# Experts 0 to 3 of a mixture of experts on one core: down-projection between the halves of the next up-projection, and GELU's rounding by halves

## The chip, the core and the metric

The kernel runs on 1 core of one Trainium2 chip. The time is the device time of one execution in microseconds (us), the median of several runs. The engines are named as in the profile: PE (TensorE; PEld are its weight loads), DVE (VectorE), ACT (ScalarE), POOL (GpSimd) and SP (SyncE, which issues most DMAs).

## The reference, cut to what matters

The output is a gated sum of two branches over the same 2048 tokens of width 448: a Fourier mixing branch, and a mixture of 8 experts of which each token takes its best 2. The change touches the expert branch alone.

```python
h = _gelu(jnp.einsum("nd,edf->nef", xt, w1))      # up-projection, F = 1792
y = jnp.einsum("nef,efd->ned", h, w2)             # down-projection
out = jnp.einsum("ne,ned->nd", cw, y)             # cw: weights of the best 2, else 0
return g * a + (1 - g) * b
```

## The kernel before

**Capacities.** Only routed tokens are computed. The experts are sorted by load, and expert e of that order gets a fixed capacity, `CAPS` = 576, 544, 544, 544, 512, 512, 512, 496 tokens. Experts 0 to 3 have more than 512, so a row of them doesn't fit one PSUM bank. They are `NQ` = 4 in number.

**Jobs.** The hidden width is cut into 14 pieces of 128, so `jobs` lists 112 pairs (e, f), f = 0 to 13, numbered u = 14 e + f. `up(u)` computes the 128 hidden features of job u for all tokens of expert e: 11 matmuls into a PSUM tile `acc`, with 32-bit values split in a rounded part (`hi`, `XH`) and what rounding left (`lo`, `XL`): XH and XL by hi, then XH by lo. Experts 0 to 3 take this in two halves of 288 (expert 0; 256 and 320 for job 0) or 272 tokens, experts 4 to 7 in one go. ACT turns each half into `g` by GELU. Then the DVE writes `gh`, g rounded (L756, a CAST), and `gl`, what that left of it (L757, a subtraction), both over the first 512 tokens at once. Of the tokens beyond 512, expert 0 writes their remainder into gh (L764), and experts 1 to 3 copy g into `rest` (L762).

`down(u)` adds job u's part to the outputs of expert e: for every tile c of 128 tokens three matmuls of 448 columns into the PSUM tile `Y[c]` (gh by `up`, gh by `dn`, gl by `up`, where up and dn are the two parts of w2's rows). Tokens beyond 512 are a fifth tile: in expert 0 two matmuls, in experts 1 to 3 `few`, which collects 6 or 8 jobs and runs 8 narrow matmuls (L807). With the last job of an expert `combine` scales each tile of Y (DVE for even c, ACT for odd) and POOL adds it to the output by an indirect DMA.

**The order.** PE, DVE, ACT and SP run their instructions in the order in which the code gives them out. The loop (L1034 to L1053) has for each u: `turn_due` (gathered tokens of the next expert into XH and XL), `prep(u + 2)` (hi and up by ACT at L205, lo and dn by DVE at L210, then the fetch of job u + 5's weights by SP), routing work in the first steps (`advance`), `stage` (transposes of gathered tokens, L646, and new gathers on POOL), then `up(u + 1)`, `down(u)`, and `side_work` (checks of the DFT matrices on the DVE at L874, blends, sends). So the PE does all of up(u + 1) and then all of down(u); job u's gh and gl are needed one step after up(u). W (hi, lo) is used by up, V (up, dn) by down. `acc` has 3 buffers, g 2, gh and gl 3.

Of the kernel before, what the change touches and what calls it, by code (L numbers as in the profile page):

```python
# [10 lines left out]
F32R = mybir.dt.float32r  # L11
# [4 lines left out]
OP = mybir.AluOpType  # L16
AX = mybir.AxisListType

P = 128
# [3 lines left out]
DX = 512  # L23
# [5 lines left out]
CMAX = max(CAPS)  # L29
FULL = 4  # L30
RMAX = CMAX - FULL * P
# [9 lines left out]
NQ = P // Q  # L41
# [21 lines left out]
def r32(ap):  # L63
    return ap.bitcast(F32)


def tiles_of(cap):
    return [min(P, cap - c * P) for c in range((cap + P - 1) // P)]
# [3 lines left out]
def tile_kernel(ctx: ExitStack, tc: tile.TileContext, xt, xrows, xplain, wg, whid, cq, cw, cspec, edge, refs, wquad, whall, cgen, wcat, out):  # L72
    nc = tc.nc
    te, ve, se, gp, sp = nc.tensor, nc.vector, nc.scalar, nc.gpsimd, nc.sync
# [3 lines left out]
    stream = ctx.enter_context(tc.tile_pool(name="stream", bufs=3))  # L78
# [85 lines left out]
    def clear(i):  # L164
        if i == 0:
            rt["zero"] = mp.tile([P, D], F32, name="yt", bufs=1)
            ve.memset(rt["zero"], 0.0)
        if i < NT + NCT:
            sp.dma_start(out[i * P : (i + 1) * P, :], rt["zero"])
# [9 lines left out]
    jobs = [(e, f) for e in range(E) for f in range(NF)]  # L179
    RAW, W, V, owner = {}, {}, {}, {}  # L180
    rt = {}
# [16 lines left out]
    def apart(e):  # L198
        return CAPS[e] - FULL * P == Q
# [16 lines left out]
    def prep(k):  # L216
        if k < len(jobs):
            upper(k)
            lower(k)
# [237 lines left out]
    def advance(n=1):  # L457
        for _ in range(n):
            next(route, None)
# [225 lines left out]
    def turn_due(e, step, lag, pace):  # L685
        c = due(e, step - lag - 1, pace)
        if c is not None:
            turn(e, c)

    def stage(e, step, lag, pace):  # L690
        c = due(e, step - lag, pace)
        if c is not None:
            blocks(e, c)
        c = due(e, step, pace)
        if c is not None:
            gather(e, c)
# [30 lines left out]
    mp = late.enter_context(tc.tile_pool(name="mp", bufs=2, side="right"))  # L727
    UP, GH, Y, REST = 0, {}, {}, {}
    last = len(jobs) - 1

    def up(u):
        e, f = jobs[u]
        hi, lo = W[u]
        cap = CAPS[e]
        rem = max(0, cap - FULL * P)
        g = mp.tile([P, CMAX], F32, name="g")
        nh = 1 if cap <= 512 else 2
        cut = 2 * P if u == 0 else cap // nh
        for hf in range(nh):
            cs = slice(hf * cut, cap if hf == nh - 1 else cut)  # L740
            n = cs.stop - cs.start
            acc = ps.tile([P, 512], F32, name="acc")
            part = lambda w, x, c: (w[:, c * P : (c + 1) * P], x[e][:, c, cs])
            steps = [part(hi, XH, c) for c in range(NC - 1)] + [part(hi, XL, c) for c in range(NC - 1)]
            steps += [part(hi, XH, NC - 1)] + [part(lo, XH, c) for c in range(NC)]
            for s, (a, b) in enumerate(steps):
                te.matmul(acc[:, :n], a, b, start=s == 0, stop=s == len(steps) - 1)  # L747
            se.activation(g[:, cs], acc[:, :n], AF.Gelu_apprx_tanh)  # L748
        if u == last:
            gh, gl = (stream.tile([P, DX], F32R, name=n) for n in ("hi", "lo"))  # L750
        else:
            gh = mp.tile([P, CMAX + RMAX], F32R, name="gh", bufs=3)
            gl = mp.tile([P, FULL * P], F32R, name="gl", bufs=3)
        main = cap - rem
        top = main if apart(e) else cap
        ve.tensor_copy(gh[:, :top], g[:, :top])  # L756
        ve.tensor_tensor(gl[:, :main], g[:, :main], r32(gh[:, :main]), OP.subtract)  # L757
        if apart(e):
            if f in LOTS:
                rt["rest"] = mp.tile([P, NF - LOTS[1], Q], F32, name="rest", bufs=2)  # L760
            REST[u] = rt["rest"][:, f - max(b for b in LOTS if b <= f)]
            ve.tensor_copy(REST[u], g[:, main:cap])  # L762
        elif rem:
            ve.tensor_tensor(gh[:, cap : cap + rem], g[:, main:cap], r32(gh[:, main:cap]), OP.subtract)  # L764
        GH[u] = (gh, gl)

    def down(*us):
        e = jobs[us[0]][0]
        tl = tiles_of(CAPS[e])
        if jobs[us[0]][1] == 0:  # L770
            for c in range(len(tl)):
                Y[c] = psy.tile([P, 512], F32, name=f"y{BANKS[c]}")
        sent = []
        turns = [(c, u) for c in range(len(tl)) for u in us]
        if len(us) == 4:
            turns[3:5] = turns[4:2:-1]
        for c, u in turns:
            f, n = jobs[u][1], tl[c]
            if c == FULL and apart(e):
                few(e, u, sent)  # L780
                continue
            m = n if c < FULL else 2 * n
            cs = slice(c * P, c * P + m)
            wh, wl = (w[:, :D] for w in V[u])
            gh, gl = GH[u]
            steps = [(gh[:, cs], wh), (gh[:, cs], wl)]
            if c < FULL:
                steps.append((gl[:, cs], wh))
            for s, (a, b) in enumerate(steps):
                te.matmul(Y[c][:m, :D], a, b, start=f == 0 and s == 0, stop=f == NF - 1 and s == len(steps) - 1)  # L790
            if f == NF - 1:
                combine(e, c, n, sent)
        for u in us:
            del W[u], V[u], GH[u]

    def few(e, u, sent):
        f = jobs[u][1]
        if f + 1 not in LOTS:
            return
        lot = range(u - f + max(b for b in LOTS if b <= f), u + 1)  # L800
        for i in range(0, len(lot), NQ):
            group = lot[i : i + NQ]
            wide = NQ // len(group)
            for j in range(NQ):
                v = group[j // wide]
                cs = slice(j % wide * (D // wide), (j % wide + 1) * (D // wide))
                te.matmul(Y[FULL][j * Q : (j + 1) * Q, cs], REST[v], RAW[v][1][:, cs], start=f < LOTS[1] and i == 0, stop=f == NF - 1 and i + NQ >= len(lot), tile_position=(0, j * Q))  # L807
        for v in lot:
            del RAW[v], REST[v]
        if f == NF - 1:  # L810
            rt["rear"] = Y[FULL], sent
# [16 lines left out]
    def combine(e, c, n, sent):  # L828
        wt = rt["wgt"][:n, e, c : c + 1]
        ys = mp.tile([P, D], F32, name="ys", bufs=NCT)  # L830
        if c == FULL:
            yt = mp.tile([P, D], F32, name="yt", bufs=1)
            ve.tensor_copy(yt[:n], Y[c][n : 2 * n, :D])
            ve.tensor_tensor(yt[:n], Y[c][:n, :D], yt[:n], OP.add)
            ve.tensor_scalar(ys[:n], yt[:n], wt, None, op0=OP.mult)
        elif c % 2 == 0:
            ve.tensor_scalar(ys[:n], Y[c][:n, :D], wt, None, op0=OP.mult)
        else:
            se.activation(ys[:n], Y[c][:n, :D], AF.Copy, scale=wt)  # L839
        scatter(e, c, n, ys, sent)  # L840
# [190 lines left out]

    advance(2)
    up(UP)
    for u in range(UP, last):  # L1034
        e, f = jobs[u]
        plan = (e + 1, f - 1, 2, 2) if e else (1, f - 6, 2, 1)
        turn_due(*plan)
        prep(u + 2)
        if u < UP + SIDE:
            advance(2)  # L1040
            clear(2 * (u - UP))
            clear(2 * (u - UP) + 1)
        if u == last - NF - 1:
            tc.keep_in_program_order(gp.drain())
        if u == UP + SIDE:
            for _ in route:
                pass
            ck = late.enter_context(tc.tile_pool(name="ck", bufs=2, side="right"))
        stage(*plan)
        up(u + 1)  # L1050
        if u < last - 3:
            down(u)
        side_work(u - UP)  # L1053
    down(*range(last - 3, last + 1))
    order.close()
    late.close()
# [63 lines left out]
    with tc.For_i(0, n_a) as j:  # L1120
# [3 lines left out]
        for h in range(2):  # L1124
            hf = full.tile([P, 2 * D], F32, name="hf")
# [133 lines left out]
```

## Time and profile before

| | us |
|---|---|
| median of 3 runs (637.31 to 637.5) | 637.49 |
| the profiled execution | 637.86 |
| its span, first to last instruction | 635.9 |
| PE busy in it | 625.9 |
| DVE busy in it | 506.9 |
| ACT busy in it | 248.5 |

The profiled execution is one run; what lies around the span in it is 637.86 - 635.9 = 1.96 us. A busy time says how long an engine had something in hand, not that it was the limit; the chain of work that ended last tells which engine set the end.

### The profile page before, as it was taken

How to read it: one execution, taken by the hardware profiler on the slowest of the kernel's cores; microseconds unless marked ns; L12 is line 12 of the kernel's file. 1: busy time of each engine (PE TensorE's matmuls, PEld its weight loads, DVE VectorE, ACT ScalarE, POOL GpSimd, SP SyncE). 2: the span in 40 equal slices, each digit the busy share in tenths (PEclk: the TensorE clock that was granted, in tenths of full speed). 3: DMA queues.
4: the chain of work that ended last, by engine and by line, in shares of the span. 5: the costliest groups of instructions: out<-in, count | busy, mean ns of one | idle time of the engine just before them, and what ended most of it. 6: DMA issues, size and time to landing. Idle time of an engine off the chain costs nothing.

```text
span 635.9 us, 11090 instructions
## 1 busy us (share of the span) xinstructions
PE 625.9 (98%) x3721; PEld 563.8 (89%) x3721; DVE 506.9 (80%) x1258; ACT 248.5 (39%) x504; POOL 205.1 (32%) x194
## 2 busy tenths in 40 slices
PE   9999999999999999999999999999999999999994
PEld 5999999998998989989899788888888888888884
DVE  7889797689987899779898799988997788555560
ACT  2553233343344434353343534433343434534440
POOL 1210074554144141443340443432331442141123
PEclk9999999999999999999999999999999999999998
DMA  8546454795766865596566767779456737766755
GB/s 346 183 149 210 155 184 140 245 238 192 237 207 160 257 226 197 197 262 196 176 243 234 229 170 244 266 234 276 136 183 195 152 115 150 166 136 145 156 74 65
DMA packets 52319, 122.78 MB, mean 193 GB/s; under 512 B 7488, under 2 KB 32208, under 8 KB 50208
## 3 DMA queue, kind: packets, MB, share of 16 engines
q1 hardware_dynamic: 40944, 101.94, 47.2%
q0 software_dynamic: 11168, 20.00, 18.2%
q8 instruction: 31, 0.51, 0.3%
q14 instruction: 32, 0.26, 0.1%
q10 hardware_dynamic: 144, 0.07, 0.0%
HBM read 105.89 MB, written 16.08 MB: 192 GB/s over the span
## 4 chain that ended last, share of the span: by engine, by line
PE 94%; issue 3%; POOL 1%; DVE 1%; POOLq 0%; ACT 0%; DVEq 0%; ACTq 0%
PE acc L747 45%; PE y L790 42%; PE y L807 1%; PE acc L512 1%; PE y L555 1%; POOL out L843 1%; PE y L474 1%; PE y L116 1%; PE acc L453 0%; POOL out L995 0%; PE acc L404 0%; PE y L669 0%; PE acc L669 0%; POOLq L1028 0%; PE acc L373 0%
## 5 line engine op out<-in xcount | busy, mean ns | idle before, releaser
L748 ACT ACTIVATE g<-acc 128x272 f32<-128x272 f32 (+4 forms) x168 | 78.0, 467 | 318.2 <-issue 178.9
L637 POOL DMA_INDIRECT xg<-xrows,piece x115 | 120.5, 1048 | 226.2 <-DVE xq L646 154.3
L790 PE MATMUL y<-up,gh 128*128 128x448 f32 (+1 forms) x458 | 167.7, 366 | 0.1
L790 PE MATMUL y<-dn,gh 128*128 128x448 f32 (+1 forms) x458 | 167.6, 366 | 0.0
L747 PE MATMUL acc<-XH,hi 128*128 128x272 f32 (+4 forms) x672 | 163.8, 325 | 0.0
L790 PE MATMUL y<-up,gl 128*128 128x448 f32 (+1 forms) x444 | 162.7, 366 | 0.0
L747 PE MATMUL acc<-XH,lo 128*128 128x272 f32 (+4 forms) x672 | 134.9, 322 | 0.0
L747 PEld LDWEIGHTS acc<-XH,hi 128*128 128x128 f32 x672 | 115.2, 188 | 11.2 <-ACT hi L205 1.8
L747 PEld LDWEIGHTS acc<-XH,lo 128*128 128x128 f32 x672 | 105.9, 188 | 8.4
L756 DVE CAST gh<-g 128x512 fp32r<-128x512 f32 (+2 forms) x111 | 48.1, 433 | 81.0 <-ACT g L748 80.6
L747 PE MATMUL acc<-XL,hi 128*128 128x272 f32 (+4 forms) x504 | 107.8, 322 | 0.0
L843 POOL DMA_INDIRECT out<-ys,tok x36 | 61.9, 1721 | 112.5 <-ACT ys L839 71.2
L790 PEld LDWEIGHTS y<-up,gh 128*128 128x128 f32 (+1 forms) x458 | 85.8, 187 | 8.1 <-issue 0.3
L790 PEld LDWEIGHTS y<-dn,gh 128*128 128x128 f32 (+1 forms) x458 | 85.8, 187 | 7.8
L874 DVE CUSTOM_DVE_ANT_0 junk<-quads 128x512 f32<-128x512 f32 x128 | 88.1, 688 | 2.2
L790 PEld LDWEIGHTS y<-up,gl 128*128 128x128 f32 (+1 forms) x444 | 83.2, 187 | 7.3
L747 PEld LDWEIGHTS acc<-XL,hi 128*128 128x128 f32 x504 | 81.0, 188 | 6.9 <-DVE XL L678 0.2
L757 DVE TENSOR_TENSOR gl<-g,gh 128x512 fp32r<-128x512 f32 (+1 forms) x111 | 76.7, 691 | 10.9 <-DVE gh L756 1.4
L210 DVE TENSOR_TENSOR lo<-raw,hi 128x512 fp32r<-128x512 f32 x112 | 77.0, 688 | 1.6 <-ACT hi L205 0.6
L205 ACT ACTIVATE hi<-raw 128x512 fp32r<-128x512 f32 x112 | 69.7, 623 | 0.0
L210 DVE TENSOR_TENSOR dn<-row,up 128x448 fp32r<-128x448 f32 x112 | 69.2, 618 | 0.0
L205 ACT ACTIVATE up<-row 128x448 fp32r<-128x448 f32 x112 | 63.5, 567 | 0.0
(263 smaller groups left out, 389.8 us busy)
## 6 DMA issues: line engine op xcount, KB each, us to landing
quads<-cq SPq DMA_DIRECT2D x16, 2048.0 KB
raw<-wcat SPq DMA_DIRECT2D x112, 256.0 KB
row<-wcat SPq DMA_DIRECT2D x112, 224.0 KB
out<-yt SPq DMA_DIRECT2D x21, 224.0 KB
xraw<-xt SPq DMA_DIRECT2D x8, 512.0 KB
out<-ot POOLq DMA_DIRECT2D x16, 224.0 KB
cw<-cw SPq DMA_DIRECT2D x4, 512.0 KB
xg<-xrows,piece POOLq DMA_INDIRECT x115
```

Source lines behind the costliest of these rows:

```text
L116: te.matmul(idle, warm[:, :P], warm, start=True, stop=True)
L205: se.activation(hi[:, : raw.shape[-1]], raw, AF.Copy)
L210: ve.tensor_tensor(lo[:, :n], raw, r32(hi[:, :n]), OP.subtract)
L474: te.matmul(LT[c][j : j + 32], wgr[:, cc, far], XR[c][:, r, cc, far, 1 - h if far else h], start=s == 0, stop=s == 3, tile_position=(0, j))
L637: st = gp.indirect_dma_start(out=xg[:, q], out_offset=None, in_=xrows, in_offset=bass.IndirectOffsetOnAxis(ap=rt["piece"][:, e, g : g + 1] ...
L747: te.matmul(acc[:, :n], a, b, start=s == 0, stop=s == len(steps) - 1)
L748: se.activation(g[:, cs], acc[:, :n], AF.Gelu_apprx_tanh)
L756: ve.tensor_copy(gh[:, :top], g[:, :top])
L757: ve.tensor_tensor(gl[:, :main], g[:, :main], r32(gh[:, :main]), OP.subtract)
L790: te.matmul(Y[c][:m, :D], a, b, start=f == 0 and s == 0, stop=f == NF - 1 and s == len(steps) - 1)
L843: st = gp.indirect_dma_start(out=out, out_offset=bass.IndirectOffsetOnAxis(ap=rt["tok"][:n, e, c : c + 1], axis=0), in_=ys[:n], in_offset= ...
L874: ve.tensor_tensor_reduce(out=junk[:, :512], in0=qd[:, a[0], a[1] * 512 : a[1] * 512 + 512], in1=qd[:, b[0], b[1] * 512 : b[1] * 512 + 512 ...
```

## The change

In steps whose up(u + 1) belongs to experts 0 to 3, the first two tiles of down(u) are given out between the two halves of up(u + 1), and the other tiles after the second half. `up` takes a function `between` for that, `down` a slice `some` of its tiles; Y is set up with the first part, and W, V and GH of the job are let go with the last. gh and gl are no longer written once after both halves of GELU, but half by half, each behind its own GELU: tokens 0 to 271 and 272 to 511 in experts 1 to 3, 0 to 287 and 288 to 575 (gl to 511) in expert 0, 0 to 255 and the rest for job 0. The tokens beyond 512 are treated as before, after the second half. Steps of experts 4 to 7 keep their order.

```diff
-    def up(u):
+    def up(u, between=lambda: None):
...
+        if u == last:
+            gh, gl = (stream.tile([P, DX], F32R, name=n) for n in ("hi", "lo"))
+        else:
+            gh = mp.tile([P, CMAX + RMAX], F32R, name="gh", bufs=3)
+            gl = mp.tile([P, FULL * P], F32R, name="gl", bufs=3)
+        main = cap - rem
+        top = main if apart(e) else cap
         for hf in range(nh):
...
             se.activation(g[:, cs], acc[:, :n], AF.Gelu_apprx_tanh)
-        if u == last:
...
-        ve.tensor_copy(gh[:, :top], g[:, :top])
-        ve.tensor_tensor(gl[:, :main], g[:, :main], r32(gh[:, :main]), OP.subtract)
+            hs, ls = slice(cs.start, min(cs.stop, top)), slice(cs.start, min(cs.stop, main))
+            ve.tensor_copy(gh[:, hs], g[:, hs])
+            ve.tensor_tensor(gl[:, ls], g[:, ls], r32(gh[:, ls]), OP.subtract)
+            if hf < nh - 1:
+                between()
...
-    def down(*us):
+    def down(*us, some=slice(None)):
...
-        if jobs[us[0]][1] == 0:
+        if jobs[us[0]][1] == 0 and not some.start:
...
-        sent = []
-        turns = [(c, u) for c in range(len(tl)) for u in us]
+        sent = rt["sent"] = [] if not some.start else rt["sent"]
+        turns = [(c, u) for c in range(len(tl))[some] for u in us]
...
-        for u in us:
-            del W[u], V[u], GH[u]
+        if some.stop is None:
+            for u in us:
+                del W[u], V[u], GH[u]
...
-        up(u + 1)
-        if u < last - 3:
-            down(u)
+        if jobs[u + 1][0] < NQ:
+            up(u + 1, lambda: down(u, some=slice(None, 2)))
+            down(u, some=slice(2, None))
+        else:
+            up(u + 1)
+            if u < last - 3:
+                down(u)
```

## Rows read from the trace of the kernel before

**Rows 1.** The page: busy us, share of the span and count of each engine, and the share of each engine in the chain that ended last.

```profile
PE 625.9 (98%) x3721; PEld 563.8 (89%) x3721; DVE 506.9 (80%) x1258; ACT 248.5 (39%) x504; POOL 205.1 (32%) x194
...
PE 94%; issue 3%; POOL 1%; DVE 1%; POOLq 0%; ACT 0%; DVEq 0%; ACTq 0%
```

**Rows 2.** The waits of the PE over the whole trace, all there are: who waited for whom, us in total, times, the longest.

```profile
PE y L116 <- DVE warm L111: 1.4, 1, 1.4
PE y L259 <- DVE mb L256: 0.5, 1, 0.5
```

**Rows 3.** The chain that ended last in order of time: start, us, what. One run of down each early and late in expert 0, one run of up and one of down in expert 2, one run of down in expert 4.

```profile
55.85 2.89 PE y L790 x14
...
110.63 2.83 PE y L790 x14
...
250.37 2.77 PE acc L747 x22
253.14 2.47 PE y L790 x12
...
401.79 2.43 PE y L790 x12
```

**Rows 4.** The timeline of the PE in a step of expert 2 (start us, us): the first matmuls of the two halves of up(38), the first and the fourth of down(37), and the first of the next up.

```profile
250.21 0.54 PE L747 MATMUL acc<-XH,hi 128*128 128x272 f32 x3
...
251.59 0.54 PE L747 MATMUL acc<-XH,hi 128*128 128x272 f32 x3
...
252.98 0.36 PE L790 MATMUL y<-up,gh 128*128 128x448 f32 x1
...
253.59 0.37 PE L790 MATMUL y<-up,gh 128*128 128x448 f32 x1
...
255.45 0.54 PE L747 MATMUL acc<-XH,hi 128*128 128x272 f32 x3
```

**Rows 5.** Busy time in a window of four steps (f = 1 to 4 of expert 2): its us, then PE, PEld, DVE, ACT and POOL busy with counts, PEclk (granted clock), DMA share, GB/s.

```profile
206.83:227.79 20.96, 20.96 (x137) 20.09 (x136) 19.18 (x49) 9.06 (x20) 6.10 (x6) 1.00 0.68 217
```

**Rows 6.** Groups of DVE instructions between 135.42 and 347.82 us, in experts 1 to 3: busy us, mean ns of one, idle time before them and what ended it.

```profile
L756 DVE CAST gh<-g 128x512 fp32r<-128x512 f32 x39 | 16.8, 430 | 20.7 <-ACT g L748 20.6
...
L762 DVE COPY rest<-g 128x32 f32<-128x32 f32 x39 | 7.8, 201 | 0.0
```

**Rows 7.** The timeline at the start of the experts: of the DVE, the rounding of job 0 (43.99 is L764, 44.13 its successor) and the CAST of job 1; of the PE, the first matmuls of the two halves of up(1) and of down(0).

```profile
42.89 0.46 DVE L756 CAST gh<-g 128x576 fp32r<-128x576 f32 x1
...
43.99 0.22 DVE L764 TENSOR_TENSOR gh<-g,gh 128x64 fp32r<-128x64 f32 x1
44.13 0.68 DVE L210 TENSOR_TENSOR lo<-raw,hi 128x512 fp32r<-128x512 f32 x1
...
48.03 0.40 DVE L756 CAST gh<-g 128x576 fp32r<-128x576 f32 x1
...
41.14 0.56 PE L747 MATMUL acc<-XH,hi 128*128 128x288 f32 x3
...
42.60 0.56 PE L747 MATMUL acc<-XH,hi 128*128 128x288 f32 x3
...
44.06 0.37 PE L790 MATMUL y<-up,gh 128*128 128x448 f32 x1
```

**Rows 8.** The timeline of expert 2, steps 29 to 33: of the DVE, the CASTs of jobs 30, 31 and 33, lo of job 34, and behind the last CAST its subtraction and the copy after it; of the PE, the start of up(34) and its first matmul with lo.

```profile
210.23 0.43 DVE L756 CAST gh<-g 128x512 fp32r<-128x512 f32 x1 [1.05 <-ACT g L748]
...
216.70 0.62 DVE L756 CAST gh<-g 128x512 fp32r<-128x512 f32 x1
...
226.79 0.69 DVE L210 TENSOR_TENSOR lo<-raw,hi 128x512 fp32r<-128x512 f32 x1
...
227.94 0.42 DVE L756 CAST gh<-g 128x512 fp32r<-128x512 f32 x1
228.46 0.69 DVE L757 TENSOR_TENSOR gl<-g,gh 128x512 fp32r<-128x512 f32 x1
229.07 0.17 DVE L762 COPY rest<-g 128x32 f32<-128x32 f32 x1
...
227.79 0.54 PE L747 MATMUL acc<-XH,hi 128*128 128x272 f32 x3
...
228.67 0.67 PE L747 MATMUL acc<-XH,lo 128*128 128x272 f32 x4
```

**Rows 9.** The timeline of expert 3, steps 43 to 47: of the DVE, the CASTs of jobs 44 and 47 and lo of job 48; of the PE, the start of up(48).

```profile
286.88 0.43 DVE L756 CAST gh<-g 128x512 fp32r<-128x512 f32 x1 [1.51 <-ACT g L748]
...
303.13 0.69 DVE L210 TENSOR_TENSOR lo<-raw,hi 128x512 fp32r<-128x512 f32 x1
...
304.27 0.42 DVE L756 CAST gh<-g 128x512 fp32r<-128x512 f32 x1
...
304.44 0.54 PE L747 MATMUL acc<-XH,hi 128*128 128x272 f32 x3
```

**Rows 10.** The timeline of expert 1, steps 17 to 19: of the DVE, the CASTs of jobs 18 and 19; of the PE, the start of up(20).

```profile
144.06 0.43 DVE L756 CAST gh<-g 128x512 fp32r<-128x512 f32 x1 [0.82 <-ACT g L748]
...
151.08 0.42 DVE L756 CAST gh<-g 128x512 fp32r<-128x512 f32 x1
...
151.14 0.54 PE L747 MATMUL acc<-XH,hi 128*128 128x272 f32 x3
```

**Rows 11.** The timeline of ACT at the end of expert 0: both GELUs of job 14, with the idle time before them.

```profile
125.03 0.69 ACT L748 ACTIVATE g<-acc 128x272 f32<-128x272 f32 x2 [7.02 <-PE y L790]
```

More of the change, by code (lines that the diff above doesn't have):

```diff
@@ L748, in up @@
             se.activation(g[:, cs], acc[:, :n], AF.Gelu_apprx_tanh)
-        if u == last:
[L750 to L755, printed above, removed]
-        ve.tensor_copy(gh[:, :top], g[:, :top])
-        ve.tensor_tensor(gl[:, :main], g[:, :main], r32(gh[:, :main]), OP.subtract)
+            hs, ls = slice(cs.start, min(cs.stop, top)), slice(cs.start, min(cs.stop, main))
[3 more added lines that the diff above has]
+                between()
         if apart(e):
```

## The prediction

> **What bounds the kernel now.** First the page's busy line and its chain: the PE is busy 98% of the span and 94% of the chain that ended last is PE work [rows 1]. Then the waits of the PE over the whole trace: two, 1.9 us together, both before the experts begin [rows 2]. So in experts 0 to 3 nothing that the PE needs comes late, and the chain in order of time shows what is left: runs of matmuls end to end. A step of experts 1 to 3 is 22 matmuls of 272 columns in 2.77 us and 12 of 448 in 2.47 us, 5.24 us in all; expert 0 has 2.92 for 22 of 288 columns and 2.89 for 14 [rows 3, 7]. The granted clock there is 1.00 of full speed, the 2.4 GHz level, and the DVE is busy 19.18 of 20.96 us in the four steps that I come back to [rows 5]. The reader should see two things: the change leaves out no matmul, so on the PE it can win only if matmuls follow each other faster in the new order; and the DVE, off the path by a little, gets more to do.
>
> I call the step in which up(u+1) and down(u) run "step u", and its start the first matmul of up(u+1) (up(34) starts at 227.79, so step 33 does).
>
> **Part 1, the order on the PE: the same 34 matmuls.** Up, 6 matmuls of down, up, the other 6 (8 in expert 0). Two more changes of shape a step. What one does shows in a step of expert 2 [rows 4]. The first half of up, which follows down, takes 251.59 - 250.21 = 1.38 us, the second 252.98 - 251.59 = 1.39. The first three matmuls of down take 253.59 - 252.98 = 0.61 us, the nine after them 255.45 - 253.59 = 1.86, 0.62 for three. So the start of a run is slightly quick, and no gap stands at either change. In the new order the second half of up also follows down (0.01 us less) and the second run of down also starts afresh (0.01 less): 0.02 us a step, over the 41 steps u = 14 to 54: **-0.8 us**. In expert 0 the two halves show no such difference (42.60 - 41.14 and 44.06 - 42.60, both 1.46 [rows 7]): nothing. Bounds: the same 448-column matmuls ran at 2.43 us for 12 in experts 4 to 7, and 2.83 for 14 late in expert 0 [rows 3]; which of the two paces a run falls into is nothing I can read from the trace. All at the quick pace: 41 x 0.04 + 9 x 0.06 = 2.2, with the halves -2.6 us. All at the slow one, the starts of runs no longer quick: 41 x 0.01 = +0.4. I take -0.8, because it is what the stretches in question themselves show.
>
> **Part 2, GELU's rounding in halves: two more DVE instructions a step.** ACT still has two GELUs. The DVE gets two CASTs (272 and 240 columns) for one of 512, and two subtractions for one. From start to start a CAST of 512 takes 228.46 - 227.94 = 0.52 us and a subtraction 229.07 - 228.46 = 0.61 [rows 8]; the subtraction's own row is longer, 0.69, so neighbours overlap. A CAST of 512 is 0.43 and a COPY of 32 is 0.20 [rows 6], so 272 columns come to about 0.31; the subtraction waits for that result, hence about 0.36 and 0.35 from start to start, 0.71 for 0.52: +0.19. The subtraction starts its successor after 0.61 for 512 and 0.13 for 64 (L764, 43.99 to 44.13 [rows 7]), so 0.35 + 0.31 for 0.61: +0.05. Together 0.24, with two more dispatches taken as **+0.27 us a step** (an estimate); bounds +0.1 (all overlapped) and +0.4 (the semaphore latencies exposed twice).
> The Trainium skill speaks against this part (VectorE: DVE Perf Modes, section "The TRN2 errata"): a fixed latency is paid by every instruction, and tiles of 512 or more should be kept so that it amortizes; its formula for a 32-bit subtraction, (N + 151) cycles at 0.96 GHz, agrees with the 0.69 us of the row. By it, with nothing overlapped, a step would cost about 0.31 us more instead of 0.27 (an estimate: twice 151 cycles), and each chain below 0.1 us more.
> All of this hides behind the PE as long as the DVE has idle time: it waits for GELU 20.6 us before the 39 CASTs between 135 and 348 us, 0.53 a step [rows 6]. So on average 0.27 fits. Where it doesn't is the question.
>
> **Part 3, where the cover is thin.** The change moves two deadlines. Tiles 0 and 1 of down(u) start one half of up earlier (1.38 instead of 2.77 into the step), and the second half of GELU arrives two tiles later (6 x 0.206 = 1.23 us). When the DVE waits for GELU, its CAST starts 3.40 into the step now (210.23 for u = 29, whose step starts at 227.79 - 4 x 5.24 = 206.83 [rows 8]) and has both instructions out after 1.13; afterwards only the second halves are left: 3.40 + 1.23 + 0.66 = 5.29 against 4.53. **The DVE is 0.75 us later behind every such wait**, and 0.27 more for each further step until its next one. Everything queued there shifts with it: the transposes and XL of the next expert, the checks of quads, and lo and dn of the weights; also SP's next raw and row fetches and POOL's gathers, which wait for buffers the DVE frees, but those have a step or more in hand. What is late first:
> - *Step 0.* The DVE starts gh(0) at 42.89, behind the routing, and down(0) needs it at 44.06; 44.06 comes after both halves of up(1), and the new order needs tile 0 after one, at 41.14 + 1.46 = 42.60 [rows 7]. A CAST of 256 lands at about 43.18, the PE starts at 43.24: 0.64 us; then gl lands at 43.68 against 43.65: 0.1. **+0.75 us** (0.6 to 0.9). Step 1 has gh from 48.03 + 0.27 against 44.06 + 2.89 + 0.75 + 1.46 = 49.2 [rows 3, 7]: nothing.
> - *Step 33* (f = 5 of expert 2). The last wait is gh(30); gh(31), gh(32), gh(33) follow without such a wait (the first starts at 216.70, the last at 227.94 [rows 8]). Shift 0.75 + 2 x 0.27 = 1.29. lo(34), 226.79 + 0.69, would land at 228.77 where the PE wants it at 228.67: 0.1. gh(33)'s first half would land at 227.94 + 1.29 + 0.31 = 229.54; the PE wants it at 227.79 + 1.38 + 0.1 = 229.27: 0.27; its gl at 230.0: 0.1. **+0.45 us** (0.1 to 0.7).
> - *Step 47* (f = 5 of expert 3) is the same place: last wait 286.88, lo(48) 303.13, gh(47) 304.27, the step starts at 304.44 [rows 9]. lo lands at 303.13 + 0.69 + 1.29 = 305.1, wanted at 304.44 + 0.88 = 305.3 (0.88 as in step 33): free. gh lands at 304.27 + 1.29 + 0.31 = 305.9, wanted at 304.44 + 1.38 = 305.8; gl 0.1 more: **+0.2 us** (0 to 0.6).
> - *Step 19* (expert 1, the same f) has its last wait at gh(18), one step before (144.06), so the shift is 0.75: gh(19), at 151.08, is done by 152.2 and wanted at 151.14 + 1.38 = 152.5 [rows 10]: free. At the end of expert 0 ACT stands idle for 7.02 us until 125.03 [rows 11], and the DVE behind it; the PE still lost next to nothing. The new order takes tile 0's scaling out of the queue earlier there; I cost it at nothing, 0.5 us if that wait falls worse.
>
> **Sum.** -0.8 + 0.75 + 0.45 + 0.2 = **+0.6 us**. The profiled execution took 637.86 us, of which the span is 635.9; the PE runs without a break from the experts to the end, so a shift in experts 0 to 3 reaches the end whole: 638.46 against it, and against the median, 637.49, **638.1 us**.
>
> **Rivals.**
> *The PE falls into the quick pace* (-2.6), and the halves overlap on the DVE (+0.1 a step), so that step 33 costs 0.15 and step 47 nothing: 637.49 - 2.6 + 0.75 + 0.15 = **635.8 us**. For: the quick pace is seen with the same shapes; a changed order is what might tip it. Against: 41 steps in a row held the slow one.
> The Trainium skill (Perfetto Trace Analysis, section "Optimization Strategy") says that where the most contended engine changes over time, interleaving the regimes can help; here up has matmuls 126 ns apart and down 206 ns apart, which may be such a pair, but three matmuls next to a change differ by 0.01 us from the rest [rows 4], so only this rival would be its gain.
> *Slower: the DVE chain is longer than I think.* If the first half's rounding is not out of the way when the second arrives (shift 1.23) and a step costs 0.4, step 33 costs 1.2, step 47 1.0, steps 19 and 20 0.3 and step 0 0.9: 3.4 - 0.8 = +2.6, **640.1 us**. It decides from a shift at lo(34) of some 1.6 us on, 0.3 above mine.
> *The change doesn't do what it says:* the halves are tracked as one tile, so that tile 0 waits for the second half's rounding as well: 0.7 more at each of the three places, **640.1 us**. For: gh and gl are one tile each. Against: gh's last columns are already written by an instruction of their own (L764).
>
> **Chances.** About 0.2% of the time, 1.27 us, is what a measurement of this kernel can tell from no change: 636.2 to 638.8. Forecast 0.48 (all within), quick pace 0.22 (faster), long chain 0.22, one tile 0.08 (both slower). Its own range by the bounds is 636.2 to 639.2; with a part of the rivals on either side, 635.4 to 640.3. Faster 0.22, same 0.48, slower 0.30.
>
> **What would show it.** A step of experts 1 to 3 should read as four pieces, 1.38, 1.23, 1.38 and 1.23 us; the waits of the PE should have a row of 0.6 to 0.9 us on gh or gl at about 43 us, and small ones near 229 and 306. The DVE's CAST count should be 55 or 56 higher, with means near 310 and 430 ns for half CASTs and half subtractions. I am wrong if the pieces of a step add up to less than 5.20 us, or if the PE waits on lo or gl over 1 us anywhere after step 0.

## The result and the profile after

The changed kernel takes 640.75 us (median of 6 runs, 639.72 to 642.3) beside 637.5 (6 runs, 637.31 to 637.69): ratio 1.0056, 95% interval 1.0046 to 1.0067. It is 3.25 us slower, where I forecast +0.6 and a range up to 640.3. The runs of the changed kernel also differ more among themselves here: 2.6 us against 0.4.

The profiled execution of it took 639.72 us (span 637.7), 1.86 more than that of before; it is the fastest of the six, so its trace shows only that much of the 3.25 us. The page's busy line, and under it all waits of the PE over the trace (who waited for whom, us in total, times, the longest; "issue": the profile shows no releaser):

```profile
PE 627.2 (98%) x3721; PEld 563.7 (88%) x3721; DVE 520.2 (82%) x1370; ACT 248.4 (39%) x504; POOL 209.0 (33%) x194
```

```profile
PE y L116 <- DVE warm L111: 1.4, 1, 1.4
PE y L793 <- issue: 0.6, 1, 0.6
PE y L793 <- DVE gh L757: 0.5, 1, 0.5
PE y L259 <- DVE mb L256: 0.3, 1, 0.3
```

Beside [rows 1, 2]: the same 3721 matmuls, 112 more DVE instructions and 13.3 us more of DVE time, a wait on gh that was foreseen, and one of 0.6 us that nothing released ("issue"), which was not. This list is too short all the same, since a matmul that starts late in the middle of a run is counted as busy. So I compared, from the two timelines, when each up(u) starts (us; the differences are of the unrounded starts):

```
            before   after   difference   what lies between
up(1)        41.14   41.03     -0.11
up(2)        46.96   47.60     +0.64      step 0: +0.75
up(10)       95.97   96.37     +0.40      steps 1 to 8: -0.24
up(11)      101.81  103.81     +2.01      step 9: +1.61
up(15)      124.66  126.78     +2.12      steps 10 to 13: +0.11
up(16)      130.18  132.01     +1.84      step 14: -0.28
up(34)      227.79  229.52     +1.73      steps 15 to 32: -0.11
up(35)      234.39  236.45     +2.06      step 33: +0.33
up(48)      304.44  306.40     +1.96      steps 34 to 46: -0.10
up(49)      311.04  313.31     +2.27      step 47: +0.31
up(56)      347.82  350.03     +2.21      steps 48 to 54: -0.06
```

Steps 0, 33 and 47 are the places of the forecast. Without step 9 the experts would have cost 2.32 - 1.61 = 0.71 us, about the +0.6 of the sum. That it comes so near is in part luck: the pace gave back 0.27 us in experts 1 to 3 for the 0.8 forecast, while expert 0, which was put at nothing, gave 0.13 and step 14 another 0.28, which the kernel before loses there behind the late GELU of [rows 11]. Step 9 is the miss. In the trace of after_again, the same kernel in a run near the median (640.88 us), it is larger: 1.05 us in step 8, inside the block L404 that stands ahead of up(10), and 1.32 in step 9.

**The foreseen waits.** The timeline (start us, us) of step 0 and of step 33, beside [rows 7, 8]:

```profile
42.77 0.29 DVE L757 CAST gh<-g 128x256 fp32r<-128x256 f32 x1
...
43.12 0.48 PE L793 MATMUL y<-up,gh 128*128 128x448 f32 x1 [0.47 <-DVE gh L757]
...
43.44 0.32 DVE L757 CAST gh<-g 128x320 fp32r<-128x320 f32 x1
...
229.51 0.69 DVE L210 TENSOR_TENSOR lo<-raw,hi 128x512 fp32r<-128x512 f32 x1
229.52 0.54 PE L754 MATMUL acc<-XH,hi 128*128 128x272 f32 x3
...
230.65 0.29 DVE L757 CAST gh<-g 128x272 fp32r<-128x272 f32 x1
...
231.00 0.47 PE L793 MATMUL y<-up,gh 128*128 128x448 f32 x1
231.05 0.44 DVE L758 TENSOR_TENSOR gl<-g,gh 128x272 fp32r<-128x272 f32 x1
...
231.31 0.36 PE L793 MATMUL y<-dn,gh 128*128 128x448 f32 x1
...
231.55 0.47 PE L793 MATMUL y<-up,gl 128*128 128x448 f32 x1
...
231.86 0.36 PE L793 MATMUL y<-up,gh 128*128 128x448 f32 x1
...
232.05 0.18 DVE L765 COPY rest<-g 128x32 f32<-128x32 f32 x1
```

In step 0 the PE starts 0.06 us behind the end of the first half's CAST and ahead of the second half's (43.44): the halves are tracked apart. In step 33 gh and gl each come a little late, and the matmul behind each late one starts 0.31 us after it where 0.21 is usual.

**The stall that was not foreseen.** The timeline of the PE in step 9, and the DVE's copy of the routing weights, which waits for it; first the changed kernel, then the kernel before, there with GELU of job 10:

```profile
94.70 1.85 PE L404 MATMUL acc<-vw,oa 128*128 128x120 bf16 x32
96.37 0.91 PE L754 MATMUL acc<-XH,hi 128*128 128x288 f32 x3
...
97.86 1.07 PE L754 MATMUL acc<-XH,lo 128*128 128x288 f32 x4
98.77 0.36 PE L793 MATMUL y<-up,gh 128*128 128x448 f32 x1
99.72 0.36 PE L793 MATMUL y<-dn,gh 128*128 128x448 f32 x1 [0.59 <-issue]
...
99.90 0.20 DVE L407 COPY wgt<-acc 128x40 f32<-128x40 f32 x1 [2.59 <-PE acc L754]
```

```profile
94.31 1.85 PE L404 MATMUL acc<-vw,oa 128*128 128x120 bf16 x32
95.97 0.64 PE L747 MATMUL acc<-XH,hi 128*128 128x288 f32 x3
...
96.97 0.69 PE L747 MATMUL acc<-XH,lo 128*128 128x288 f32 x4
97.50 0.56 PE L747 MATMUL acc<-XH,hi 128*128 128x288 f32 x3
...
98.93 0.20 DVE L407 COPY wgt<-acc 128x40 f32<-128x40 f32 x1 [3.53 <-PE acc L747]
...
99.11 0.71 ACT L748 ACTIVATE g<-acc 128x288 f32<-128x288 f32 x2 [5.58 <-PE acc L747]
```

In the changed kernel the 11 matmuls of up(10)'s first half take 98.77 - 96.37 = 2.40 us, where they took 1.53 before (97.50 - 95.97), and the second matmul of down waits 0.95. No semaphore stands behind it: the matmuls that start late (96.75, 97.51, 98.27 and 99.72) and their weight loads name none to wait for. L404's result is done at 96.55 by its row, but the DVE's copy, which waits for it, starts at 99.90, just after the PE goes on at 99.72. The kernel before shows only this second side: its block L404 ends at 96.16 and the first half of up(10) at 97.66, yet the DVE and ACT, idle and waiting for just these, start at 98.93 and 99.11. What the PE finished was reported 1.4 to 2.8 us late there too (the profile models the ends of matmuls, but it is not that far off: halves_only, below, has 0.04), while its matmuls went on.

### The profile page after: what moved, and what is told of

It reads as the page before. It is cut to its first block, busy times and chain, and to the rows that moved or that the text cites. A ratio compares the mean times of both kernels' runs of the same rounds, so it can differ in the third digit from the quotient of the medians.

```text
span 637.7 us, 11202 instructions
## 1 busy us (share of the span) xinstructions
PE 627.2 (98%) x3721; PEld 563.7 (88%) x3721; DVE 520.2 (82%) x1370; ACT 248.4 (39%) x504; POOL 209.0 (33%) x194
## 5 line engine op out<-in xcount | busy, mean ns | idle before, releaser
L637 POOL DMA_INDIRECT xg<-xrows,piece x115 | 124.1, 1079 | 228.4 <-DVE gh L757 94.2
L754 PEld LDWEIGHTS acc<-XH,hi 128*128 128x128 f32 x672 | 118.6, 188 | 13.4 <-issue 2.0
L757 DVE CAST gh<-g 128x272 fp32r<-128x272 f32 (+5 forms) x167 | 57.2, 343 | 70.4 <-ACT g L755 68.4
L758 DVE TENSOR_TENSOR gl<-g,gh 128x272 fp32r<-128x272 f32 (+6 forms) x167 | 85.9, 514 | 12.1 <-issue 0.5
```

Source lines behind the costliest of these rows:

```text
L637: st = gp.indirect_dma_start(out=xg[:, q], out_offset=None, in_=xrows, in_offset=bass.IndirectOffsetOnAxis(ap=rt["piece"][:, e, g : g + 1] ...
L757: ve.tensor_copy(gh[:, hs], g[:, hs])
L758: ve.tensor_tensor(gl[:, ls], g[:, ls], r32(gh[:, ls]), OP.subtract)
```

## The experiments

Rows of one letter ran on one chip, beside runs of the kernel before on that chip; there were five chips, A to E; which chips the two profiles above came from is not known. The times are medians, the ratio is over all runs.

| chip | kernel | us | before | ratio (95%) |
|---|---|---|---|---|
| A | order_only | 640.55 | 637.34 | 1.0049 (1.0035 to 1.0063) |
| A | halves_only | 637.53 | 637.34 | 1.0003 (0.9994 to 1.0012) |
| A | experts_1_to_3 | 638.08 | 637.34 | 1.0014 (1.0005 to 1.0023) |
| A | expert_0 | 638.11 | 637.34 | 1.0015 (1.0006 to 1.0024) |
| B | after_again | 640.91 | 637.71 | 1.0064 (1.0048 to 1.0080) |
| B | old_0 | 640.21 | 637.71 | 1.0038 (1.0025 to 1.0051) |
| B | old_9 | 640.43 | 637.71 | 1.0056 (1.0040 to 1.0072) |
| B | old_0_33_47 | 639.79 | 637.71 | 1.0033 (1.0020 to 1.0046) |
| C | after_third | 639.89 | 637.30 | 1.0042 (1.0028 to 1.0056) |
| C | expert_0_second | 638.71 | 637.30 | 1.0025 (1.0015 to 1.0034) |
| C | experts_1_to_3_second | 638.56 | 637.30 | 1.0022 (1.0013 to 1.0031) |
| C | clears_early | 638.58 | 637.30 | 1.0020 (1.0011 to 1.0029) |
| D | clears_in_9 | 640.35 | 637.95 | 1.0039 (1.0025 to 1.0052) |
| D | before_clears_in_9 | 637.55 | 637.95 | 0.9995 (0.9986 to 1.0004) |
| D | before_clears_early | 637.73 | 637.95 | 0.9998 (0.9989 to 1.0007) |
| D | clears_early_old | 639.68 | 637.95 | 1.0028 (1.0016 to 1.0040) |
| E | block_later | 644.31 | 637.91 | 1.0103 (1.0088 to 1.0118) |
| E | two_of_block | 643.34 | 637.91 | 1.0070 (1.0051 to 1.0090) |

### The two parts, one at a time (chip A)

order_only: gh and gl in one piece behind the second half.

```diff
-            ve.tensor_copy(gh[:, hs], g[:, hs])
-            ve.tensor_tensor(gl[:, ls], g[:, ls], r32(gh[:, ls]), OP.subtract)
             if hf < nh - 1:
                 between()
+        ve.tensor_copy(gh[:, :top], g[:, :top])
+        ve.tensor_tensor(gl[:, :main], g[:, :main], r32(gh[:, :main]), OP.subtract)
```

> The new order of the PE alone; gh and gl are written once after both halves of GELU, as before. Theory A (single stalls of the PE make the loss: 0.77 us in step 0, 0.34 each in steps 33 and 47, and 2 us or more in step 9, about 96 to 100 us, where the PE waits for no semaphore; pace -0.5): the stall of step 0 grows to about 1.1, step 9 stays, so 639.5 to 640.5 us. Theory B (the new order is a little slower on the PE in every step): 640 to 641 as well, but the pieces of a step are longer than 1.38 and 1.23 us. Theory C (the loss is the DVE's added instructions): 637.5 to 638.3 us.

+3.2 us. By the starts of up(u), as in the table above, step 0 costs 1.17 us, step 19 0.76, step 33 0.56 and step 47 0.54, together 3.0; the pace and step 14 give some 0.5 of it back. The 0.7 left of the median's difference I can't place. Step 19, where halves were in time, shows how (the DVE's two instructions, and the PE's matmuls that wait for them):

```profile
153.45 0.42 DVE L758 CAST gh<-g 128x512 fp32r<-128x512 f32 x1
...
153.92 0.47 PE L792 MATMUL y<-up,gh 128*128 128x448 f32 x1
153.97 0.69 DVE L759 TENSOR_TENSOR gl<-g,gh 128x512 fp32r<-128x512 f32 x1
154.23 0.36 PE L792 MATMUL y<-dn,gh 128*128 128x448 f32 x1
154.72 0.47 PE L792 MATMUL y<-up,gl 128*128 128x448 f32 x1
```

So theory C falls, and the halves are worth having once the order is new: they remove 0.4 us of step 0, all of step 19 and 0.2 each of 33 and 47. This profile has no stall in step 9: the time fits theory A, but longer waits stand where it put the stall.

halves_only: the condition of the new order is `False`.

> GELU's rounding and residual by halves alone; the PE's order as before. Theory A: nothing is needed earlier than before, 637.3 to 637.8 us. Theory B: the same. Theory C (added DVE instructions make the loss): 639 us or more, with waits of the PE on gh, gl or lo.

No difference that can be measured, with all 112 DVE instructions added: the DVE's idle time does hide them, as long as gh is not needed early.

experts_1_to_3 and expert_0: both parts, under a condition on the expert.

```diff
-        if jobs[u + 1][0] < NQ:
+        if 0 < jobs[u + 1][0] < NQ:      # expert_0: == 0; the halves under the same condition
```

> Both parts, but only where up(u + 1) belongs to experts 1 to 3; expert 0 as before. Theory A: steps 0 and 9 are as before, so 0.34 + 0.34 - 0.3 (41 steps by 0.007 us): 637.5 to 638.2 us. Theory B (each step a little slower): 42 of 55 steps are changed, so three quarters of the loss stays, about 640 us. Theory C: about 640 us too.

> Both parts, but only where up(u + 1) belongs to expert 0. Theory A: step 0 (0.77 us) and step 9 (2 us or more) with a gain of about 0.3 in pace: 639.5 to 641 us, and a larger spread from run to run than the kernel before has (0.4 us). Theory B: a quarter of the loss, about 638.3 us. Theory C: about 638.3 us.

+0.74 and +0.77 us. The first fits theory A. The second has the time that B and C gave, but all of it in one place, step 0 (0.74 us by the starts of up): neither is borne out, and theory A wanted the stall of step 9, of which the profile has none. Here up(10)'s first half behind the block takes 1.50 us (the chain that ended last, in order of time: start, us, what):

```profile
96.49 1.50 PE acc L754 x11
```

The two losses add up to 1.5 us, half of the whole change's, which was never run on this chip. And chip A differs from the others in another way, which its traces show: nothing is reported late there. halves_only, the same place as above:

```profile
94.77 1.85 PE L404 MATMUL acc<-vw,oa 128*128 128x120 bf16 x32
...
96.66 0.20 DVE L407 COPY wgt<-acc 128x40 f32<-128x40 f32 x1 [1.24 <-PE acc L404]
```

The copy starts 0.04 us after the block's end. In the four traces of chip A no GELU that ACT stands idle for starts more than 0.4 us behind the end of its matmuls; in each of the other sixteen, the kernel before among them, 5 to 11 start more than 0.6 us late. So a trace of chip A without a stall says nothing of the order of the code.

### Is the stall the change's or one execution's? (chip B)

after_again is the changed kernel as it is; the other three have single steps in the old order, with the halves kept:

```diff
-        if jobs[u + 1][0] < NQ:
+        if jobs[u + 1][0] < NQ and u > 0:                  # old_9: u != 9
+        if jobs[u + 1][0] < NQ and u not in (0, 33, 47):   # old_0_33_47
```

> The changed kernel once more. Expert 0 alone cost 0.77 us and experts 1 to 3 alone 0.74, so the parts add up to 638.9 us beside 637.35 before. Theory A (the stall of 2 us in step 9 belongs to the changed kernel): 640.5 to 641 us again, and the profile shows PE without a semaphore wait at about 96 to 100 us again. Theory D (that stall is an event of single executions, not of the order of the code): 638.6 to 639.2 us, with no stall in step 9.

> The changed kernel, with step 0 alone in the old order of the PE (GELU's rounding stays in halves). Both theories: 0.75 to 0.85 us below the changed kernel, since the wait on gh(0) at 42.4 us goes; what follows is queued the same. Theory A: about 640.0 us, theory D: about 638.1 us.

> The changed kernel, with step 9 alone in the old order of the PE. Theory A (the new order in the step behind the block of L404 makes the PE stall): 2 us below the changed kernel. Theory D: the same time as the changed kernel within 0.3 us.

> The changed kernel, with steps 0, 33 and 47 in the old order of the PE: the three places where the PE waits on gh or gl. Theory D: 0.77 + 0.34 + 0.34 = 1.45 us below the changed kernel, 637.2 to 637.6 us: no gain is left but the 0.3 to 0.5 of the pace. Theory A: 639.3 us, the stall of step 9 being still there. If waits come up at the neighbours (steps 32, 34, 46, 48) instead, up to 0.5 us more.

Theory D falls: +3.2 us again, and all four profiles have a stall between 96 and 100 us. The three foreseen waits are worth 1.12 us together (640.91 - 639.79), where 1.45 was expected, and step 0 alone 0.70 for 0.75 to 0.85; by the starts of up in old_0_33_47, step 1 loses 0.33 us once step 0 has the old order, which is the rest of the 1.45. With all three gone 2.1 us over the kernel before are left. old_9 stalls as well, so the stall doesn't need the new order in step 9 itself. The profiled run of old_0 (642.19 us, 2 above its median) shows what else a stall may bring (busy time by windows: its us, PE, PEld, DVE, ACT, POOL with counts, granted clock, DMA share, GB/s):

```profile
98.00:100.00 2.00, 1.11 (x9) 0.89 (x8) 0.51 (x4) 0.00 (x0) 0.22 (x1) 1.00 0.97 338
100.00:102.00 2.00, 2.00 (x7) 1.80 (x7) 1.87 (x9) 0.41 (x1) 0.00 (x0) 0.51 0.08 26
```

The PE had stood still for 1.01 us until 97.75 and for 0.89 until 99.19, and then the granted clock fell to about half, the 1.2 GHz level: the matmuls of down start 0.37 us apart, where 0.21 is usual. This makes the loss differ from run to run: in the changed kernel's six runs the mean granted clock is 0.993 and 0.994 in the two slowest (642.3 and 641.8 us) and 0.996 to 0.998 in the other four.

### Whole and parts on one chip, and the clears (chip C)

after_third, expert_0_second and experts_1_to_3_second are the kernels of those names; clears_early:

```diff
-            clear(2 * (u - UP))
-            clear(2 * (u - UP) + 1)
+            for k in range(3):
+                clear(3 * (u - UP) + k)
```

> The changed kernel, beside its two halves on the same chip. The runs with a part of the change alone came from one chip, those of the whole change from others; in the traces of the first chip no PE stall stands at 96 to 100 us, in all five of the others one does, in one of them with the granted clock at half behind it. Theory E (the stall of step 9 goes with the chip or its state, not with the amount of the change): where this run shows the stall, the kernel with expert 0 alone shows it too, and the sum of the two halves' losses is the whole loss, about 3.2 us; where it doesn't, the whole loss is about 1.5 us. Theory F (the stall needs the whole change): this one 640.5 to 641 us and the two halves 638.1 us each, as they were.

> Both parts of the change in expert 0 only, beside the whole change on the same chip. Theory E: whatever stall after_third shows in step 9, this kernel shows too, so it is 0.4 to 0.8 us below that kernel. Theory F: 638.1 us and no stall in step 9, with 640.5 or more for the whole change.

> Both parts in experts 1 to 3 only, on the same chip as the whole change. Both theories: 0.3 to 0.8 us over the kernel before, from the waits of steps 33 and 47 less what the pace gives back; step 9 has its old order here and shows no stall of the PE, as in the kernel before.

> The changed kernel, with the 21 clears of the output on SP's queue given out three a step in steps 0 to 6 instead of two in steps 0 to 10, so that none falls in step 9, where 448 KB of them stand beside the weights and the gathers just when the PE stalls. If that traffic makes the stall: 2 us below the whole change where it stalls (about 638.9 us), no stall between 95 and 101 us. If not: the same time as the whole change within 0.4 us.

Whole +2.59, parts +1.41 and +1.26: together 2.67, so the parts add up here, as theory E says. On A they came to 1.51; the intervals of each part on the two chips overlap, so it is the traces, which stall here and not there, that speak for the chip. In step 9 after_third loses 0.67 us by the starts of up, expert_0_second 0.35, clears_early 0.07. experts_1_to_3_second shows a different loss, at the end of expert 0 (ACT's GELUs of job 14, the CASTs behind them, and the PE's first matmul of down(14)):

```profile
124.17 0.40 ACT L755 ACTIVATE g<-acc 128x272 f32<-128x272 f32 x1 [6.79 <-PE y L798]
124.61 0.30 DVE L759 CAST gh<-g 128x272 fp32r<-128x272 f32 x1 [5.35 <-ACT g L755]
124.99 0.40 ACT L755 ACTIVATE g<-acc 128x272 f32<-128x272 f32 x1
...
126.03 0.47 PE L798 MATMUL y<-up,gh 128*128 128x448 f32 x1 [0.45 <-DVE ys L846]
```

GELU comes late because the PE's matmuls are reported late, as in [rows 11] (here they ended at 119.97), and the DVE's scaling of tile 0 (`ys`), which the PE waits for, is queued behind the CAST and the subtraction; the PE loses 0.7 us at 126.03, where it lost 0.3 in step 14 of the kernel before (the starts at 127.30 and 127.64 are followed 0.34 and 0.31 us later, for 0.13 and 0.21). clears_early looked like the cure: 1.3 us less than the whole change, and no stall.

### It was not the clears (chip D)

clears_in_9 deals two clears a step to steps 0 to 7 and five to step 9; before_clears_in_9 and before_clears_early do the two things to the kernel before; clears_early_old joins clears_early and old_0_33_47.

```diff
-            clear(2 * (u - UP))
-            clear(2 * (u - UP) + 1)
+            for i in range(2 * (u - UP), 2 * (u - UP) + 2) if u - UP < 8 else range(16, 21) if u - UP == 9 else ():
+                clear(i)
```

> The changed kernel with the clears dealt out two a step in steps 0 to 7, none in steps 8 and 10, and five (1120 KB) in step 9 instead of two. Theory G (the traffic of that step stalls the PE): the stall at 96 to 101 us grows, 640.5 to 643 us, over 0.5 above the whole change. Theory H (taking the clears out helped for another reason, such as a shift of when things are issued): within 0.4 us of the whole change, 639.9 to 640.9 by the chip.

> The kernel before with five clears in step 9 (none in 8 and 10). If the traffic stalls the PE in any order: 1 us or more above the kernel before, with a stall at 95 to 101 us. If the old order rides it out because nothing on the PE waits for that step's results within a step: 637.2 to 637.7 us.

> The kernel before with all clears in steps 0 to 6. The PE lost nothing at step 9 there, so both theories: the same as the kernel before within 0.3 us, 637.0 to 637.6. If the clears cost the kernel before as well in the runs that left no profile: 0.4 us or more below it.

> The changed kernel with all clears in steps 0 to 6 and steps 0, 33 and 47 in the old order. With the stall of step 9 gone and 1.1 to 1.45 us of waits on gh gone from 638.6: 637.1 to 637.5 us, that is no faster than the kernel before, as the pace gives back only 0.3 to 0.5 us and the stall at the end of expert 0 may take it. If a gain of the order is hidden under the stalls: below 636.8 us.

Theory G falls twice. Five clears in place of two gave +2.4 us, no more than the whole change on chip C. And clears_early_old, with no clear in step 9, stalls there again (1.90 us by the starts of up) and takes 639.68 us instead of 637.1 to 637.5. The kernel before is moved by neither dose. No version here beats it.

### It was not the burst of short matmuls (chip E)

block_later puts two more `yield`s ahead of the block L404, so that it comes one step later; two_of_block leaves out 30 of its 32 matmuls, and with them most of the sum that makes the routing weights, so its output is not the kernel's.

```diff
         yield
+        yield
+        yield
         acc = ps.tile([P, 512], F32, name="acc")
         for p in range(NP):
-            te.matmul(acc[:, : 3 * MAIN], oa[:, p], vw[:, p], start=p == 0, stop=p == NP - 1)
+            if p in (0, NP - 1):    # two_of_block, without the yields
+                te.matmul(acc[:, : 3 * MAIN], oa[:, p], vw[:, p], start=p == 0, stop=p == NP - 1)
```

> The changed kernel with the block of 32 bf16 matmuls (L404), and the routing work behind it, one step later. Theory I (the burst of short matmuls brings the stall): no stall at 96 to 100 us, one of 0.3 to 2 us within 3 us behind the block's new place near 102 us. Theory J (what else happens at 96 to 100 us, gathers and weight fetches, brings it): the stall stays at 96 to 100 us in step 9. The time is 639.9 to 640.9 us under both, or 1 to 2 us less if the place alone was unlucky.

> The changed kernel with 2 of the 32 matmuls of the block L404; the other 30 are left out, so the routing weights, and with them the output, lack most of their terms. The block took 1.66 us, of which some 1.55 go: theory I: no stall in step 9, 1.55 + 0.7 to 2 us below the whole change, 636.5 to 638.6 us. Theory J: the stall stays, 638.3 to 639.4 us, and the profile shows it at about 95 to 98.5 us.

Both became slower, by 6.4 and 5.4 us over the kernel before. block_later stalls inside the block at its new place, three times about 1.05 us, the second of them with the DMAs at a share of 0.17; two of the windows, with the columns as above, stand below it, the second with the clock at half behind the stalls:

```profile
100.64 1.03 PE L406 MATMUL acc<-vw,oa 128*128 128x120 bf16 x16
102.73 0.37 PE L406 MATMUL acc<-vw,oa 128*128 128x120 bf16 x4 [1.07 <-issue]
104.15 0.42 PE L406 MATMUL acc<-vw,oa 128*128 128x120 bf16 x5 [1.04 <-issue]
105.59 0.55 PE L406 MATMUL acc<-vw,oa 128*128 128x120 bf16 x7 [1.02 <-issue]
```

```profile
103.00:105.00 2.00, 0.53 (x7) 0.34 (x5) 0.34 (x2) 0.82 (x2) 0.95 (x1) 1.00 0.17 45
...
107.00:109.00 2.00, 2.00 (x9) 2.00 (x9) 1.83 (x9) 0.01 (x1) 0.00 (x0) 0.50 0.45 117
```

two_of_block has no stall at 96 to 100 us, but three at 100.8 to 105.8 us that the profile lays to no releaser (0.83, 0.34 and 0.26 us idle; the weight loads at the end of the first and the last do name a semaphore, of ACT and of the PE itself), and then one that it lays to the DVE:

```profile
105.79 0.41 ACT L756 ACTIVATE g<-acc 128x288 f32<-128x288 f32 x1 [3.88 <-remote]
...
112.65 0.50 PE L794 MATMUL y<-up,gh 128*128 128x448 f32 x1 [2.10 <-DVE gh L758]
```

GELU of up(10) came so late (its second half's matmuls ended at 99.47) that the DVE's whole queue, routing work included, ran late behind it, and gh came 2.1 us late; then the clock stood at 0.50 here too (113.5 to 115.5 us). So theory I falls as it was put (the stall doesn't need the burst), and J too (with the block moved, nothing stalled at 96 to 100 us); but in block_later a stall went where the block went.

## Why the prediction was wrong

**The step that failed** is the one ahead of the sum: "the PE runs without a break from the experts to the end", with "nothing that the PE needs comes late" in front of it. I took it from the list of waits, which knows a wait only by its semaphore, and looked for thin cover on the DVE alone. [rows 11] already showed another engine late for a reason that was not the DVE: ACT idle for 7.02 us until the PE's matmuls were reported. I costed it at nothing. In the runs this region, from the routing's last block to the end of expert 0, holds what I missed: 1.61 us in step 9 of the profiled execution, 2.37 in steps 8 and 9 of after_again, 2.1 us on chip B after the foreseen waits are gone, 0.7 at 126 us in experts_1_to_3_second.

**What is shown of it and what is not.** Shown: where reports come late, the stall comes with the new order in the steps of expert 0. All sixteen traces other than those of chip A have the late reports. The four of them with the old order in expert 0 (before, experts_1_to_3_second, both of before with moved clears) don't stall in step 9. Of the twelve with the new order eleven do: eight by 0.67 us or more (step 9 with the block L404 ahead of it), among them old_9, whose step 9 has the old order; expert_0_second by 0.35; block_later in the moved block, behind down(9), and two_of_block from there on. Only clears_early runs through. On chip A there are neither late reports nor stalls, in either order. In the nine traces that stall at 96 to 100 us the two also end together: the DVE's copy of the late result starts 0.12 to 0.23 us after the PE has gone on. So the stall comes only with late reports, but a late report alone is no stall. Not the cause by themselves: the clears, the amount of traffic (block_later's windows; halves_only has a DMA share of 0.76 to 1.04 from 96 to 99 us and no late report), the block's 32 matmuls. What makes the reports late, and what holds the PE up for a microsecond without a semaphore, stays open. One rival no run tests: that recording the trace has a part in it. The sixteen traces lack about a tenth of the semaphore records (the changed kernel has 421 for the PE's 467), those of chip A none.

**The waits on gh.** Step 0: +0.75 us, as forecast. Step 33: 0.33 for 0.45, step 47: 0.31 for 0.2. The DVE's shift at gh(33) is 1.13 - 0.15 = 0.98 us (its start less the step's, 230.65 - 229.52 and 227.94 - 227.79 [rows 8]), not 1.29; at gh(47), in the same way (307.53 - 306.40 = 1.13, and 304.27 - 304.44 = -0.17 [rows 9]), 1.30, as forecast. What I left out is the restart: the matmul behind a late one starts 0.1 us later than usual, twice in each step, which made up for the smaller lateness in 33 and was the excess in 47. Step 19 was free, as forecast.

**The DVE's term** was right: from the first CAST to the copy of `rest` 232.05 - 230.65 = 1.40 us, against 229.07 - 227.94 = 1.13 [rows 8]: +0.27. The Trainium skill (VectorE: DVE Perf Modes, section "The TRN2 errata") would have it at about 0.31 with nothing overlapped (an estimate: twice the 151 cycles of its formula, which it gives for an add); the rows of the halves bear out that fixed part (two CASTs of 287 and 292 ns for one of 430 [rows 6]: 149 more, where 151 cycles at its 0.96 GHz are 157), and the overlap takes some of it back. The groups of the same stretch as [rows 6] (busy us, mean ns, idle before):

```profile
L758 DVE TENSOR_TENSOR gl<-g,gh 128x272 fp32r<-128x272 f32 x39 | 17.5, 448 | 4.3 <-issue 0.5
...
L757 DVE CAST gh<-g 128x240 fp32r<-128x240 f32 x40 | 11.7, 292 | 11.6 <-ACT g L755 11.0 <-issue 0.4
L757 DVE CAST gh<-g 128x272 fp32r<-128x272 f32 x39 | 11.2, 287 | 0.6 <-ACT g L755 0.4
```

287 and 448 ns for the 310 and 430 expected, and the wait for GELU ahead of the CASTs went from 20.6 us to 11.4: the cover paid for it.

**The pace** was mis-sized. I took 0.02 us a step; four steps of expert 2 take 20.93 us (208.59 to 229.52) for 20.96 [rows 5], 0.007 a step, since the second half of up, which now follows down too, still takes 1.39 us, and only down, with its second start, gained (chain of clears_early in expert 2, where no wait breaks it):

```profile
244.52 1.23 PE y L793 x6
245.75 1.38 PE acc L754 x11
247.13 1.23 PE y L793 x6
248.36 1.39 PE acc L754 x11
```

Over experts 1 to 3, steps 15 to 54 without 33 and 47, that is -0.27 us by the table for -0.8. The quick pace did not come: a run of six stays at 1.23 us.

**The rivals.** The long DVE chain gave 640.1 us, near the result, but for a reason that didn't happen: its shift would have had to pass 1.6 us at lo(34), and it was 0.99 (229.51 - 229.52 against 226.79 - 227.79 [rows 8]). That the halves are one tile falls with step 0's rows (its own sum, 0.6 and three times 0.7, makes 640.2 us, not 640.1). The forecast's own range doesn't come out of the bounds of its terms either: these add up to -1.9 and +2.6, 635.6 to 640.1 us, for the 636.2 to 639.2 given.

## What to carry to other kernels

A list of waits without entries says that no semaphore came late, not that the engine has slack: compare the starts of like pieces of work between two traces, step by step, and let the sum of the differences show what the list leaves out. An engine that stands idle for work that another one finished long ago, by its own rows, is a warning: here it stood in every trace in which a new order stalled, and cost the kernel before 0.3 us. A version that stalls less on one chip (clears_early) shows a cause only after the dose and the combination have been tried; and versions are compared on one chip, since one of five had neither the late reports nor the stall.

## What was not expected of the hardware

- The PE stopped between matmuls without a semaphore, for 0.2 to 1.2 us beyond the usual from start to start (1.02 to 1.07 us idle three times in block_later), and the place and size changed from trace to trace; on chip A it did not.
- In the kernel before, results of the PE were reported 1.4 us (GELU at 99.11, matmuls ended at 97.66) and 4.4 us late (GELU at 125.03, whose matmuls ended at 120.59) while the PE ran on; on chip A none came over 0.4 us late.
- Behind stalls of about 1 us the granted clock read 0.50 to 0.51 (the 1.2 GHz level) in old_0, block_later and two_of_block; in old_0 step 9 lost 4.08 us, of which the stalls are 2.5.
- A matmul that waits for its operand costs the next one as well: 0.31 us from start to start for the usual 0.21.
